# Where the expert's operands lie in on-chip memory: weights and token parts of an attention and mixture kernel moved into pools of their own

## The chip, the cores and the metric

The kernel runs on one core of a Trainium2 chip. The metric is the device time of one execution in microseconds (us), lower is better. The engines are TensorE (PE in the views; its weight loads are a row of their own, PEld), VectorE (DVE), ScalarE (ACT), GpSimd (POOL) and SyncE (SP), which only issues transfers.

## The reference: what is computed

Two stages, all in float32. The first is attention over 8 batches, 8 heads, 576 positions and 64 features: one attention over positions pooled by four, repeated back up, plus a banded attention (three neighbours to each side). The second stage takes the result as 4608 tokens of 512 features and computes a gated expert:

```python
x_prev = np.concatenate([np.zeros((B, 1, D)), x[:, :-1, :]], axis=1)
xk = mu_k * x + (1.0 - mu_k) * x_prev
xr = mu_r * x + (1.0 - mu_r) * x_prev
k = np.maximum(xk @ w_k, 0.0)          # 512 -> 1024
v = k * k @ w_v                        # 1024 -> 512
r = 1.0 / (1.0 + np.exp(-(xr @ w_r)))  # 512 -> 512
return (r * v).astype(np.float32)
```

The weights arrive as float64; the kernel reads them as pairs of 32-bit words.

## The kernel before

**Splitting into two parts.** The three products of the expert are done on PE in a 4-byte format (float32r). To keep the accuracy of float32 each operand is split into a high part and a low part (what the high part leaves over), and three products are added: high by high, high by low, low by high. A weight tile holds both parts: 2 x 512 elements of each partition, 4096 bytes, high part first. There are twenty of them: wk0 to wk7 (half c of the 1024 columns of w_k by 128-row block p, index 4c + p), wv0 to wv7, wr0 to wr3. They stay on the chip for the whole run. The token parts are made anew for each chunk: xkh and xkl, xrh and xrl (mixed tokens, 4 x 256 elements, 4096 bytes), and kh and kl (the squared activations of one 128-column block f, 256 elements, 1024 bytes).

**Chunks and units.** The 4608 tokens are taken in 18 chunks of 256 (c = 0 to 17). For a chunk PE does three kinds of units:

- a k unit (k_pe, L669, matmul at L674), one for each f = 0 to 7: 12 matmuls, p = 0 to 3 by three products. The loaded (stationary) operand is a 128x128 piece of a wk tile, the streamed (moving) operand is 256 columns of xkh or xkl. Units f = 0 to 3 use wk0 to wk3, units f = 4 to 7 use wk4 to wk7.
- an r unit (r_pe, L699, matmul at L704), two for a chunk: 12 matmuls with a 128x128 piece of xrh or xrl loaded and 512 columns of a wr tile streamed.
- a v unit (v_pe, L713, matmul at L719), one for each f: 6 matmuls with a 128x128 piece of kh or kl loaded and 512 columns of wv streamed.

So a chunk has 96 matmuls of 256 columns and 24 + 48 of 512 columns. Each matmul has a weight load of its own, which runs while the matmul before it streams; at any moment PE thus streams one tile and loads from another.

Within a steady chunk the units come in this order: k1 r0 r1 k2 k3 v0 v1 k4 v2 k5 v3 k6 v4 k7 v5 v6 v7, with k0 of the next chunk put ahead of v6 (list UNITS, L30, and L843). Behind a k unit ACT takes the relu, the square and the high part (L679, L685, L686), and DVE or POOL the low part (L693), before the v unit of the same f.

**Attention.** Between those units stand the attention's matmuls of the 32 head pairs (run_pe, L590), in float32, which end near 600 us. The first stage of the program, up to about 120 us, loads and splits the weights (weight_scale to weight_low, L281 to L323), does the first attention pairs, and fills idle PE time with dummy matmuls (keep_warm, L310 to L315, both operands from the tile nidn).

**Order.** A planner written into the kernel (class Plan, L45 to L214) orders all tasks by costs and due times, and the order on each engine is fixed by manual dependencies (in_order, L926).

**Where tiles lie.** A tile pool lays its tiles down one behind another in the order in which their tags are first used, in steps of 32 bytes, and pools stand in the order in which they are opened. There are two on-chip pools before: const (masks, the identity and the like) and work (everything else, weights and token parts among them). The small tiles between the weights (for instance mxd with 12 bytes, which takes 32) set where each one starts. Every operand piece that PE loads or streams starts a multiple of 512 bytes into its tile, so that what matters of an address below multiples of 512 is that of its tile.

Of the kernel before, what the change touches and what calls it, by code (L numbers as in the profile page):

```python
# [7 lines left out]
F32 = mybir.dt.float32  # L8
F32R = mybir.dt.float32r
# [8 lines left out]
P = 128  # L18
NP = H // 2
NF = DFF // P  # L20
CT = 256
# [195 lines left out]
@with_exitstack  # L217
def attention_moe(ctx: ExitStack, tc, q, k, v, mu_k, mu_r, w_k, w_v, w_r, band, ident, out):
    nc = tc.nc
    cp = ctx.enter_context(tc.tile_pool(name="const", bufs=1))  # L220
    wp = ctx.enter_context(tc.tile_pool(name="work", bufs=2))
    pp = ctx.enter_context(tc.tile_pool(name="psum", bufs=2, space=PSUM))
# [44 lines left out]
        return (wr if kind == "r" else wv)[i * P:(i + 1) * P, :]  # L267

    def weight_tile(key, shape, dt):
        return wp.tile([P] + shape, dt, tag="w" + key, name="w" + key, bufs=1)  # L270

    def w_k_part(p, f, h):
        c, f = divmod(f, NP)
# [2 lines left out]
    def fetch_weight(i):  # L276
        raws[i] = weight_tile(WORDER[i], [512, 2], I32)
        nc.sync.dma_start(raws[i], weight_source(WORDER[i]).rearrange("p (n w) -> p n w", w=2))
# [20 lines left out]
    def weight_high(i):  # L299
        ws[WORDER[i]] = weight_tile(WORDER[i], [2, 512], F32R)  # L300
        nc.scalar.activation(ws[WORDER[i]][:, 0, :], part32[i], AF.Copy)
# [355 lines left out]
            nc.vector.tensor_tensor(out=x[:, :, o:o + L], in0=x[:, :, o:o + L], in1=xts[b][:, :, s:s + L], op=ALU.add)  # L657

    def mix_high(c, nm):
        h = wp.tile([P, NP, CT], F32R, tag=nm + "h", name=nm + "h", bufs=2 if nm == "xk" else 1)  # L660
        nc.scalar.activation(h, mixes[c][nm], AF.Copy)
        xs[c, nm] = [h]

    def mix_low(c, nm):
        lo = wp.tile([P, NP, CT], F32R, tag=nm + "l", name=nm + "l", bufs=2 if nm == "xk" else 1)
        nc.vector.tensor_tensor(out=lo, in0=mixes[c][nm], in1=xs[c, nm][0].bitcast(F32), op=ALU.subtract)  # L666
        xs[c, nm].append(lo)

# [12 lines left out]

    def k_high(c, f):
        kk = kq[c, f]
        kh = wp.tile([P, CT], F32R, tag="kh", name="kh", bufs=4)
        nc.scalar.activation(kk, kk, AF.Square)  # L685
        nc.scalar.activation(kh, kk, AF.Copy)  # L686
        kq[c, f] = kk, kh

    def k_low(c, f):
        kk, kh = kq[c, f]  # L690
        eng = nc.gpsimd if low_on(c, f) == "POOL" else nc.vector
        kl = wp.tile([P, CT], F32R, tag="kl", name="kl", bufs=4)
        eng.tensor_tensor(out=kl, in0=kk, in1=kh.bitcast(F32), op=ALU.subtract)  # L693
        kq[c, f] = kh, kl

    def low_on(c, f):
        return "POOL" if c < KLPOOL or f in KLF else "DVE"
# [122 lines left out]
    def chunk(c):  # L820
# [5 lines left out]
        for nm, o in (("xk", 0), ("xr", 5)):  # L826
            src = f"xk32{c}" if nm == "xk" else f"dx{c}"
            for p in range(NP):

                add(*(("ACT", 0.49) if act_mix(c) else ("DVE", 0.48 * len(segs(c)))), X + o + 1 + 0.5 * p, mix_part, c, nm, (p,),  # L830
                    r=xt + [f"dx{c}", "mu"] + ([f"xkh{c}"] if nm == "xr" and c < ACTMIX else []),
                    new=[(src, "f32tmp")] if nm == "xk" and p == 0 else [], w=[src] if nm == "xr" or p else [])
            if act_mix(c):
                add("DVE", 1.22, X + o + 2.5, mix_add, c, nm, r=xt, w=[src])
            add("ACT", 1.04, X + o + 3, mix_high, c, nm, r=[src], new=[(f"{nm}h{c}", nm + "h")])
            add("DVE", 1.22, X + o + 4, mix_low, c, nm, r=[src, f"{nm}h{c}"], new=[(f"{nm}l{c}", nm + "l")])
# [7 lines left out]
        for f in range(NF):  # L844
            W = where[f"k{f}"]
            if f == NP:

                while held:
                    held.pop(0)()
            add("PE", 1.43, W, k_pe, c, f, r=[f"xkh{c}", f"xkl{c}"] + both(f"k{4 * (f // 4) + p}" for p in range(NP)),  # L850
                new=[(f"g{c}.{f}", "bank")])
            add("ACT", 0.38, W - 6, k_relu, c, f, r=[f"g{c}.{f}"], new=[(f"kk{c}.{f}", "kk")])
            add("ACT", 0.82, W - 6, k_high, c, f, w=[f"kk{c}.{f}"], new=[(f"kh{c}.{f}", "kh")])
            add(low_on(c, f), 0.42 if low_on(c, f) == "DVE" else 0.74, W - 6, k_low, c, f, r=[f"kk{c}.{f}", f"kh{c}.{f}"], new=[(f"kl{c}.{f}", "kl")])
# [126 lines left out]
```

## Time and profile before

| | us |
|---|---|
| median of three runs | 704.89 (704.68 to 708.3) |
| the profiled execution | 705.88 |
| its span, first to last instruction | 703.9 |
| PE busy within the span | 674.1 (96%) |
| PE weight loads (PEld) | 576.9 (82%) |
| DVE, ACT, POOL busy | 465.5, 439.3, 303.3 |

A matmul's record is longer than its share of PE's time, because matmuls overlap in the pipeline: one of 512 columns is recorded with 389 to 397 ns, but the next starts some 227 to 236 ns after it. What a matmul costs in a run of them is therefore read from one start to the next, not from its mean duration. In the chain of waits a piece "x12 1.43" is a run of 12 matmuls that took 1.43 us from the first start to the next piece. PEclk is the granted clock of PE in tenths of full speed; over the span it is 0.992.

### The profile page before, as it was taken

Reading aid. Unit: us, or ns where it says so; the run is one execution under the profiler, and the core shown is the slowest. Engines: PE = TensorE matmul, PEld = TensorE weight load, DVE = VectorE, ACT = ScalarE, POOL = GpSimd, SP = SyncE. Lnnn points to the kernel's source line nnn. Section 1 sums busy time; section 2 is a strip of 40 time slices with the busy share of each in tenths; the row PEclk is TensorE's granted clock in tenths of the full one; section 3 lists DMA queues with packets and bytes.
Section 4 is the critical chain, followed back from the end, with each engine's and each line's share of the span. In section 5 each row is a group of like instructions: output and inputs, shape, how many; then the busy total and the mean of one; then the engine's idle time right before and its main releaser. Section 6 shows DMA issues by size and latency. Waiting matters only on the chain.

```text
span 703.9 us, 18635 instructions
## 1 busy us (share of the span) xinstructions
PE 674.1 (96%) x7467; PEld 576.9 (82%) x7467; DVE 465.5 (66%) x855; ACT 439.3 (62%) x1095; POOL 303.3 (43%) x374
## 2 busy tenths in 40 slices
PE   7888977999999999999999999999999999999997
PEld 5565866888888888888888888888888888988986
DVE  4778987659965977498753996488748963555111
ACT  3557864777757765667665667585758575744432
POOL 5535898656453646345341555455544521000000
PEclk9999998999999999999999999999999999999999
DMA  8899997635353426242351364334351100000000
GB/s 149 181 197 273 221 148 132 124 79 116 68 114 75 107 56 128 54 93 44 87 87 52 59 115 88 88 77 104 71 101 40 53 2 31 1 30 31 1 32 31
DMA packets 221849, 62.21 MB, mean 88 GB/s; under 512 B 205122, under 2 KB 214594, under 8 KB 221762
## 3 DMA queue, kind: packets, MB, share of 16 engines
q1 hardware_dynamic: 221762, 61.01, 42.0%
q8 instruction: 59, 0.97, 0.6%
q14 instruction: 28, 0.23, 0.1%
HBM read 51.55 MB, written 9.44 MB: 87 GB/s over the span
## 4 chain that ended last, share of the span: by engine, by line
PE 69%; DVE 11%; ACT 5%; SPq 4%; POOL 4%; DMA 3%; issue 3%; DVEq 0%; POOLq 0%; ACTq 0%
PE ps_g L674 24%; PE acc L719 22%; PE ps_r L704 12%; PE ps_v L581 3%; SPq L335 3%; PE ps_a L449 2%; PE ps_v L575 2%; DMA v<-in_v_dram 1%; ACT ad L533 1%; ACT L533 1%; DVE ps_w L291 1%; PE ps_a L516 1%; DMA wv<-in_moe_w_v_dram 1%; DVE kl L693 1%; PE ps_a L509 1%
## 5 line engine op out<-in xcount | busy, mean ns | idle before, releaser
L674 PE MATMUL ps_g<-xkh,wk 128*128 128x256 f32 x1152 | 229.5, 285 | 2.9 <-ACT kk L679 2.0
L674 PEld LDWEIGHTS ps_g<-xkh,wk 128*128 128x128 f32 x1152 | 186.6, 190 | 11.4 <-ACT kk L679 4.9
L719 PE MATMUL acc<-wv,kh 128*128 128x512 f32 x576 | 181.2, 396 | 0.0
L674 PE MATMUL ps_g<-xkl,wk 128*128 128x256 f32 x576 | 162.6, 282 | 0.7 <-DVE xkl L666 0.7
L693 DVE TENSOR_TENSOR kl<-kk,kh 128x256 fp32r<-128x256 f32 x119 | 64.0, 538 | 118.0 <-ACT kh L686 110.8
L719 PEld LDWEIGHTS acc<-wv,kh 128*128 128x128 f32 x576 | 101.0, 189 | 18.9 <-issue 2.5
L674 PEld LDWEIGHTS ps_g<-xkl,wk 128*128 128x128 f32 x576 | 109.9, 191 | 3.9 <-DVE xkl L666 0.9
L719 PE MATMUL acc<-wv,kl 128*128 128x512 f32 x288 | 112.6, 391 | 0.1
L679 ACT ACTIVATE kk<-ps_g 128x256 f32<-128x256 f32 x144 | 54.5, 379 | 84.2 <-PE ps_g L674 77.9
L704 PE MATMUL ps_r<-wr,xrh 128*128 128x512 f32 x288 | 90.2, 394 | 1.7 <-POOL wr L323 1.4
L693 POOL TENSOR_TENSOR kl<-kk,kh 128x256 fp32r<-128x256 f32 x25 | 18.5, 742 | 124.2 <-PE acc L719 96.1
L719 PEld LDWEIGHTS acc<-wv,kl 128*128 128x128 f32 x288 | 54.1, 188 | 12.8 <-DVE kl L693 0.8
L686 ACT ACTIVATE kh<-kk 128x256 fp32r<-128x256 f32 x144 | 60.2, 418 | 4.6
L685 ACT ACTIVATE kk<-kk 128x256 f32<-128x256 f32 x144 | 60.1, 418 | 4.5
L704 PEld LDWEIGHTS ps_r<-wr,xrh 128*128 128x128 f32 x288 | 52.5, 188 | 12.4 <-POOL wr L323 1.8
L477 POOL TENSOR_TENSOR sm<-sm,mx 128x384 f32<-128x384 f32 x28 | 24.4, 873 | 83.1 <-DVE sd L539 60.6
L704 PE MATMUL ps_r<-wr,xrl 128*128 128x512 f32 x144 | 56.1, 390 | 0.0
L523 DVE TENSOR_REDUCE mxd<-ps_a 128x3 f32<-128x432 f32 x32 | 19.3, 604 | 48.8 <-PE ps_a L449 39.6
L422 POOL TENSOR_TENSOR v<-v 72x512 f32<-72x512 f32 x32 | 44.6, 1395 | 16.0 <-DMA v<-in_v_dram 15.8
L423 POOL TENSOR_TENSOR vd<-v 72x256 f32<-72x256 f32 x32 | 27.7, 866 | 51.0 <-PE ps_v L575 49.6
L413 POOL TENSOR_TENSOR tk<-kz 64x288 f32<-64x288 f32 (+1 forms) x56 | 41.9, 748 | 16.1 <-DVE kz L386 12.5
L533 ACT ACTIVATE ad<-ps_a,mxd 128x144 f32<-128x144 f32 x96 | 35.3, 376 | 20.3 <-DVE mxd L524 17.5
(106 smaller groups left out, 1212.5 us busy)
## 6 DMA issues: line engine op xcount, KB each, us to landing
vw<-in_v_dram SPq DMA_DIRECT2D x126, 96.0 KB
qraw<-in_q_dram SPq DMA_DIRECT2D x128, 72.0 KB
kraw<-in_k_dram SPq DMA_DIRECT2D x128, 72.0 KB
v<-in_v_dram SPq DMA_DIRECT2D x32, 288.0 KB
out_dram<-sig SPq DMA_DIRECT2D x36, 256.0 KB
wk<-in_moe_w_k_dram SPq DMA_DIRECT2D x8, 512.0 KB
wv<-in_moe_w_v_dram SPq DMA_DIRECT2D x8, 512.0 KB
wr<-in_moe_w_r_dram SPq DMA_DIRECT2D x4, 512.0 KB
```

Of the source, the lines that this page charges most:

```text
L413: nc.gpsimd.tensor_tensor(out=tk[h], in0=k4[:, :, 0:2], in1=k4[:, :, 2:4], op=ALU.add)
L422: eng.tensor_tensor(out=v4[:, :, 0:128], in0=v4[:, :, 0:128], in1=v4[:, :, 128:256], op=ALU.add)
L423: eng.tensor_tensor(out=vd, in0=v4[:, :, 0:64], in1=v4[:, :, 64:128], op=ALU.add)
L477: nc.gpsimd.tensor_tensor(out=s3, in0=s3, in1=mx[:, :, None].broadcast_to([P, 12, 32]), op=ALU.subtract)
L533: nc.scalar.activation(ad[:, t, :], ps[:, t, :], AF.Exp, scale=1.0 / 128, bias=mx[:, t:t + 1], accum_out=sd[:, t:t + 1])
L674: nc.tensor.matmul(ps, w_k_part(p, f, w), y[:, p, :], start=(m == 0), stop=(m == len(mm) - 1))
L679: nc.scalar.activation(kk, kq[c, f], AF.Relu)
L685: nc.scalar.activation(kk, kk, AF.Square)
L686: nc.scalar.activation(kh, kk, AF.Copy)
L693: eng.tensor_tensor(out=kl, in0=kk, in1=kh.bitcast(F32), op=ALU.subtract)
L704: nc.tensor.matmul(ps, y[:, p, P * t:P * t + P], ws[f"r{p}"][:, w, :], start=(m == 0), stop=(m == len(mm) - 1))
L719: nc.tensor.matmul(accs[c][t], x[:, P * t:P * t + P], ws[f"v{f}"][:, w, :], start=(f == 0 and m == 0), stop=(f == NF - 1 and m == 2))
```

## The change

Two pools are opened ahead of the others. The pool array holds the twenty weight tiles and nothing else, 20 x 4096 bytes. The pool tokens begins with an unused tile of 16 elements (64 bytes), and holds the token parts xkh, xkl, xrh, xrl, kh and kl. All other tiles stay in const and work, which now come behind. Numbers of buffers, shapes and all computation stay; on all five engines the instructions stand in the same order, with the same waits.

```diff
 def attention_moe(ctx: ExitStack, tc, q, k, v, mu_k, mu_r, w_k, w_v, w_r, band, ident, out):
     nc = tc.nc
+    ap = ctx.enter_context(tc.tile_pool(name="array", bufs=1))
+    xp = ctx.enter_context(tc.tile_pool(name="tokens", bufs=1))
+    xp.tile([P, 16], F32, name="shift")
     cp = ctx.enter_context(tc.tile_pool(name="const", bufs=1))
     wp = ctx.enter_context(tc.tile_pool(name="work", bufs=2))
...
     def weight_tile(key, shape, dt):
-        return wp.tile([P] + shape, dt, tag="w" + key, name="w" + key, bufs=1)
+        return ap.tile([P] + shape, dt, tag="w" + key, name="w" + key, bufs=1)
...
     def mix_high(c, nm):
-        h = wp.tile([P, NP, CT], F32R, tag=nm + "h", name=nm + "h", bufs=2 if nm == "xk" else 1)
+        h = xp.tile([P, NP, CT], F32R, tag=nm + "h", name=nm + "h", bufs=2 if nm == "xk" else 1)
...
     def mix_low(c, nm):
-        lo = wp.tile([P, NP, CT], F32R, tag=nm + "l", name=nm + "l", bufs=2 if nm == "xk" else 1)
+        lo = xp.tile([P, NP, CT], F32R, tag=nm + "l", name=nm + "l", bufs=2 if nm == "xk" else 1)
...
     def k_high(c, f):
-        kh = wp.tile([P, CT], F32R, tag="kh", name="kh", bufs=4)
+        kh = xp.tile([P, CT], F32R, tag="kh", name="kh", bufs=4)
...
     def k_low(c, f):
-        kl = wp.tile([P, CT], F32R, tag="kl", name="kl", bufs=4)
+        kl = xp.tile([P, CT], F32R, tag="kl", name="kl", bufs=4)
```

What this does to the addresses, in bytes past a multiple of 128 (before and after, as the two programs place their tiles):

| tiles | before | after |
|---|---|---|
| wk0, wk1, wk2 | 32 | 0 |
| wk3 to wk7, wv0 to wv7, wr0 to wr3 | 96 | 0 |
| xkh, xkl, xrh, xrl, kh, kl | 96 | 64 |
| mixed tokens before the split (dx, xk), and kk | 96 | 32 |
| idn, nidn | 0 | 64 |
| the attention's tiles | various | each moved by 64 |

The distance from a token part to the weight that it meets was 0 bytes (modulo 128) for all pairs but those with wk0, wk1 and wk2, where it was 64; it is now 64 for all. The distance between any two of the tiles that did not change pools is the same as before, modulo 128.

## The prediction

> **What bounds the kernel now.** The page first.
>
> ```profile
> span 703.9 us, 18635 instructions
> PE 674.1 (96%) x7467; PEld 576.9 (82%) x7467; DVE 465.5 (66%) x855; ACT 439.3 (62%) x1095; POOL 303.3 (43%) x374
> PE   7888977999999999999999999999999999999997
> PEclk9999998999999999999999999999999999999999
> ```
>
> PE is full in nearly every slice, at full clock. The view by stretches says from when, and the view of PE's waits what interrupts it after 120 us.
>
> ```profile
> 74.00:120.00 46.00, 36.88 (x593) 31.16 (x595) 38.06 (x57) 30.57 (x81) 41.07 (x44) 0.96 0.96 166
> 120.00:200.00 80.00, 78.65 (x981) 67.73 (x975) 61.16 (x114) 57.80 (x146) 47.58 (x59) 0.98 0.48 99
> 200.00:300.00 100.00, 98.35 (x1153) 85.01 (x1145) 69.01 (x132) 66.52 (x172) 48.81 (x60) 1.00 0.43 89
> 300.00:400.00 100.00, 100.00 (x1005) 87.82 (x1004) 70.23 (x128) 65.03 (x158) 37.09 (x46) 1.00 0.34 71
> ```
>
> ```profile
> PE ps_g L674 <- ACT kk L679: 2.0, 3, 0.8
> PE ps_t L556 <- POOL ad L544: 1.0, 2, 0.7
> ```
>
> Columns of the first are the stretch, its length, then busy time of PE, PEld, DVE, ACT and POOL. Before 120 us PE waits for loads and other engines (36.88 busy of 46). From 200 us it is busy 98 to 100 of 100, and after 120 us its longest waits sum to 2.0 and 1.0 us. So from 120 us on, a nanosecond off each matmul is a nanosecond off the end, and the question is what a matmul costs from one start to the next. The chain of waits has it for a chunk late in the program, where no attention stands between the units.
>
> ```profile
> 619.47 5.45 PE ps_r L704 x24
> 624.92 2.80 PE ps_g L674 x24
> 627.72 2.75 PE acc L719 x12
> 630.47 1.43 PE ps_g L674 x12
> 631.91 1.39 PE acc L719 x6
> ...
> 641.75 1.42 PE ps_g L674 x12
> 643.18 2.73 PE acc L719 x12
> 645.91 1.42 PE ps_g L674 x12
> 647.33 0.23 PE ps_r L704
> ```
>
> Left out are three more pairs like those at 630.47 and 631.91 (k5 to k7, v3 to v5). The chunk lasts 647.33 - 619.47 = 27.86 us: k units 2.80 + 4 x 1.43 + 2 x 1.42 = 11.36 (118.3 ns for each of 96 matmuls), r units 5.45 (227.1 ns for each of 24), v units 2.75 + 4 x 1.39 + 2.73 = 11.04 (230.0 ns for each of 48). Together 27.85.
>
> **The trial that stands in the trace already.** Units k0 to k3 load wk0, wk1 and wk2, which lie 64 bytes (modulo 128) from the streamed xkh and xkl; wk3 to wk7 lie at distance 0. So before has both layouts on the same line. The timeline of PE over k2 and k3 of the last chunk, those matmuls alone that stream xkl (one for each block p, so three matmuls from one to the next):
>
> ```profile
> 680.60 0.28 PE L674 MATMUL ps_g<-xkl,wk 128*128 128x256 f32 x1
> ...
> 681.30 0.28 PE L674 MATMUL ps_g<-xkl,wk 128*128 128x256 f32 x1
> 681.66 0.28 PE L674 MATMUL ps_g<-xkl,wk 128*128 128x256 f32 x1
> 682.02 0.28 PE L674 MATMUL ps_g<-xkl,wk 128*128 128x256 f32 x1
> ...
> 682.70 0.28 PE L674 MATMUL ps_g<-xkl,wk 128*128 128x256 f32 x1
> ```
>
> and over k4, with the first matmuls of the v unit behind it:
>
> ```profile
> 686.14 0.28 PE L674 MATMUL ps_g<-xkl,wk 128*128 128x256 f32 x1
> ...
> 687.22 0.28 PE L674 MATMUL ps_g<-xkl,wk 128*128 128x256 f32 x1
> ...
> 687.46 0.63 PE L719 MATMUL acc<-wv,kh 128*128 128x512 f32 x2
> 687.93 0.39 PE L719 MATMUL acc<-wv,kl 128*128 128x512 f32 x1
> ```
>
> In k4, at distance 0, nine matmuls take 1.08 us: 120 ns each. In k2, at distance 64, six take 0.70 us: 117 ns. Where k2 comes to wk3 (681.30 to 682.02) six take 0.72: 120 ns again. In k3, distance 64 as in k2, six take 0.68: 113.3 ns. So the distance between what is loaded and what is streamed does show, on PE, at full clock; distance 64 is never slower here than distance 0; and at distance 64 there are two rates, 117 and 113.3, of which I cannot say what selects them (k3 comes behind the disturbance by wk3, k2 comes behind r1 with none).
>
> A rule speaks against the change. The Trainium skill, page "TensorE: Matmul & The Clock Gate", section "Step-by-step: what each phase is for", says that PE reads the streamed operand and the loaded one through two independent read ports, so that loading the next weights takes nothing from the running matmul. By it both distances cost the same and the sum would be 0. The rows of k2 to k4 disagree: 113.3 to 117 against 120 ns.
>
> **The change part by part.** No instruction, byte or wait is added, taken or moved; only addresses differ.
>
> *k units.* 96 matmuls of a chunk, now 118.3 ns in the mean. After, all are at distance 64. Ends from the rows above: 113.3 (10.88 us, -0.48 for a chunk) and 117.5, the rate of k2 with its rounding (11.28, -0.08). Both rates occur, and with wk3 gone the disturbance behind which 113.3 was seen is gone too, so I take the middle, 115.4: 11.08, -0.28.
>
> *v units.* 48 matmuls. The rows give 2.73 for twelve behind k0, which loads mostly at distance 64 (227.5 ns), and 1.39 for six behind k4 to k7 (231.7). The start of a v unit pays for the state in which the k unit leaves PE: at 687.46 two matmuls take 0.47, 235 each. Ends: unchanged (0) and r's rate of 227.1 for all (10.90, -0.14). With the k units before them out of the 120 ns rate I take 227.5: 10.92, -0.12.
>
> *r units.* 24 matmuls at 227.1, with few disturbances: 0.
>
> *Which bytes.* The pieces start at 0 and 64 now, at 32 and 96 before. Alignment alone: the dummy matmuls have both operands in nidn, at 0 and at distance 0.
>
> ```profile
> 66.50:73.30 6.80, 6.80 (x32) 5.63 (x31) 1.00 1.05 131
> ```
>
> 32 of them touch 6.80 us; each is recorded with 0.39, so the spacing is about 7.19 / 32 = 225 ns (218 to 232 with one more or fewer), like r's 227.1 at 96. Aligned starts alone give nothing; I take 0.
>
> *The other engines* find their tiles moved by 64, token parts excepted. Nothing in the trace shows what this does to them, so it is bounded by their cover. Behind a k unit these follow before its v unit:
>
> ```profile
> L693 DVE TENSOR_TENSOR kl<-kk,kh 128x256 fp32r<-128x256 f32 x119 | 64.0, 538 | 118.0 <-ACT kh L686 110.8
> L679 ACT ACTIVATE kk<-ps_g 128x256 f32<-128x256 f32 x144 | 54.5, 379 | 84.2 <-PE ps_g L674 77.9
> L686 ACT ACTIVATE kh<-kk 128x256 fp32r<-128x256 f32 x144 | 60.2, 418 | 4.6
> L685 ACT ACTIVATE kk<-kk 128x256 f32<-128x256 f32 x144 | 60.1, 418 | 4.5
> ```
>
> 379 + 418 + 418 + 538 = 1.75 us, and between the end of k4 (631.91) and v4 (two v units and two k units later, 2 x 1.39 + 2 x 1.43) lie 5.64. A tenth on each of them, either way, is hidden. Without that cover, 0.17 us for each of eight units would be 1.4 us a chunk.
>
> *The sum.* -0.28 - 0.12 = -0.40 us for a chunk. Chunk 0 lies largely in the stretch up to 120 us where PE waits anyway; of the other 17 I count 16, since PE's idle 1.35 and 1.65 us between 120 and 300 show places where DVE, ACT or POOL come last and take back a part. 16 x 0.40 = 6.4 us: the span goes from 703.9 to 697.5, the profiled time from 705.88 to 699.5. That execution lies 1.0 above the median, and the same difference from the median of 704.89 gives **698.5**. Ends of the mechanism: all at the best rates, 17 x (0.48 + 0.14) = 10.5, 694.4; k2's rate and v as now, 16 x 0.08 = 1.3, 703.6.
>
> **The rivals.** *Weak form:* every k unit is entered as k2 is, at 117, and v keeps its starts: 703.6. For it: k2's rate holds over its whole undisturbed part. Against: v behind k0 is already better than behind k4. *Nothing changes,* 704.9: two independent ports, as the skill's rule has it; the difference between k2, k3 and k4 would then come from where the units stand in a chunk. Against it: within k2 the step to wk3 alone brings 120. *Slower:* the 512-column matmuls. Distance 0 is what r and v have now, and r settles at 227.1; no row shows a run of them at distance 64. If the collision that k2 shows is a matter of phase, distance 64 could hold r and v in the state that now marks only the start of a v unit, 235 ns. Then 72 x 0.235 = 16.92 against 5.45 + 11.04 = 16.49, +0.43, with k at 117.5 -0.08: +0.35 x 16 = +5.6, 710.5. It decides from 233 ns in the mean on: 229.0 now, 1.1 for k's gain, 3.0 for 3.5 us. Against: the matmuls that today load wk0 while streaming wv or wr (the last of a v or r unit ahead of k0 to k2) stand in pieces of 2.73 and 5.45 that are the shortest of their kind.
>
> **How the numbers follow.** A measurement of this kernel tells about 0.5%, 3.5 us, from no change: faster is below 701.4, slower above 708.4. The forecast, by more than that, 0.58; the weak form 0.18; nothing 0.12; the slower one 0.12, with a price between 0 and 710.5 and beyond, of which 0.02 stays within the bound. Faster 0.58, same 0.32, slower 0.10. The range of 8 in 10 reaches from 692, 2.4 below the best end since chunk 0 and rates below 113.3 may add a little, to 706, which takes in the weak form, no change and the mild part of the slower one.
>
> **What would show it.** In the profile after: twelve matmuls of a k unit in the chain at 1.36 to 1.41 instead of 1.43, the same for k0 to k3 as for k4 to k7; single v units at 1.36 to 1.37 instead of 1.39; 24 of r still 5.45; a late chunk 27.2 to 27.8 instead of 27.86; PE still 98 to 100 of 100 after 200 us. Wrong would be: k units at 1.41 and more throughout (weak form), k4 to k7 still at 1.43 (nothing), r above 5.5 (slower), or a gain in the chunks that does not reach the end because PE's waits grow.

## The result, and the profile after

The changed kernel is slower: median 709.76 us (707.25 to 712.65, 20 runs) against 705.65 for the kernel before (703.76 to 708.3, 20 runs), ratio 1.0057 (95% interval 1.0044 to 1.007). The forecast of 698.5 had the wrong sign, and the time lies above the range (692 to 706).

The page of the changed kernel first; lines of its code stand three further down than before (k units L677, r L707, v L722).

```profile
span 707.4 us, 18635 instructions
PE 680.0 (96%) x7467; PEld 577.6 (82%) x7467; DVE 465.4 (66%) x855; ACT 439.5 (62%) x1095; POOL 303.7 (43%) x374
L696 DVE TENSOR_TENSOR kl<-kk,kh 128x256 fp32r<-128x256 f32 x119 | 64.3, 540 | 119.4 <-ACT kh L689 112.1
```

DVE, ACT and POOL are as busy as before to within 0.4 us, and the last operation behind a k unit takes the same (538 ns before, 540 now). PE's busy time alone grew, by 5.9 us. The chain of waits over the late chunk, as it was shown of before:

```profile
622.16 5.60 PE ps_r L707 x24
627.76 2.82 PE ps_g L677 x24
630.58 2.80 PE acc L722 x12
633.39 1.41 PE ps_g L677 x12
634.80 1.40 PE acc L722 x6
...
646.05 2.80 PE acc L722 x12
...
650.26 0.93 PE ps_r L707 x4
```

The chunk takes 650.26 - 622.16 = 28.10 us instead of 27.86. By kind of unit:

| | before | forecast | after | a matmul after |
|---|---|---|---|---|
| k, 96 matmuls | 11.36 | 11.08 | 2.82 + 6 x 1.41 = 11.28 | 117.5 ns |
| r, 24 | 5.45 | 5.45 | 5.60 | 233.3 ns |
| v, 48 | 11.04 | 10.92 | 2.80 + 4 x 1.40 + 2.80 = 11.20 | 233.3 ns |
| chunk | 27.85 | 27.45 | 28.08 | |

The k units gained 0.08, the r units lost 0.15 and the v units 0.16. The 0.24 us of the chunk's own starts, times the 17 chunks after 120 us, are 4.1 us, as large as the difference of the medians (709.76 - 705.65 = 4.1). That they agree to the tenth is in part luck: the two profiled executions differ by 3.5 us, and the chunks with attention between their units lose less than the late one.

Summed in both traces over the starts of all matmuls from r0 of chunk 2 to r0 of chunk 17 (15 chunks), k units take 1.6 us less than before, r units 2.0 more, v units 2.4 more and the attention's matmuls the same to within 0.1: 2.9 us in all, 0.20 for a chunk. The remaining 0.5 us of the span lies ahead of and behind these chunks. PE's waits after 120 us, as the view lists them, sum to 4.3 us against 3.4 before; between r0 of chunk 2 and r0 of chunk 17 no more time goes into late starts than before.

### The profile page after: what moved, and what is told of

It is laid out like the page before. It is cut to its first block, busy times and chain, and to the rows that moved or that the text cites. A ratio compares the mean times of both kernels' runs of the same rounds, so it can differ in the third digit from the quotient of the medians.

```text
span 707.4 us, 18635 instructions
## 1 busy us (share of the span) xinstructions
PE 680.0 (96%) x7467; PEld 577.6 (82%) x7467; DVE 465.4 (66%) x855; ACT 439.5 (62%) x1095; POOL 303.7 (43%) x374
## 4 chain that ended last, share of the span: by engine, by line
PE 77%; DVE 7%; ACT 5%; POOL 4%; SPq 3%; issue 2%; DMA 1%; DVEq 0%; POOLq 0%; ACTq 0%
PE ps_g L677 25%; PE acc L722 25%; PE ps_r L707 13%; PE ps_v L584 3%; PE ps_a L452 3%; PE ps_v L578 2%; SPq L338 2%; ACT ad L536 1%; DMA v<-in_v_dram 1%; ACT L536 1%; PE ps_a L519 1%; PE ps_a L512 1%; PE ps_t L559 1%; DVE ps_w L294 1%; PE ps_t L560 1%
## 5 line engine op out<-in xcount | busy, mean ns | idle before, releaser
L677 PE MATMUL ps_g<-xkh,wk 128*128 128x256 f32 x1152 | 227.8, 284 | 3.8 <-ACT kk L682 2.2
L677 PEld LDWEIGHTS ps_g<-xkh,wk 128*128 128x128 f32 x1152 | 185.2, 189 | 12.7 <-ACT kk L682 4.9
L722 PE MATMUL acc<-wv,kh 128*128 128x512 f32 x576 | 183.6, 400 | 0.0
L677 PE MATMUL ps_g<-xkl,wk 128*128 128x256 f32 x576 | 161.2, 280 | 0.7 <-DVE xkl L669 0.7
L722 PEld LDWEIGHTS acc<-wv,kh 128*128 128x128 f32 x576 | 101.2, 189 | 20.5 <-issue 2.6
L722 PE MATMUL acc<-wv,kl 128*128 128x512 f32 x288 | 114.5, 398 | 0.0
L677 PEld LDWEIGHTS ps_g<-xkl,wk 128*128 128x128 f32 x576 | 108.7, 189 | 4.6 <-DVE xkl L669 0.9
L707 PE MATMUL ps_r<-wr,xrh 128*128 128x512 f32 x288 | 91.6, 398 | 1.8 <-POOL wr L326 1.1
L722 PEld LDWEIGHTS acc<-wv,kl 128*128 128x128 f32 x288 | 54.3, 188 | 13.6 <-DVE kl L696 0.3
L707 PEld LDWEIGHTS ps_r<-wr,xrh 128*128 128x128 f32 x288 | 52.4, 188 | 13.9 <-POOL wr L326 1.5
L707 PE MATMUL ps_r<-wr,xrl 128*128 128x512 f32 x144 | 56.9, 395 | 0.0
```

The costliest lines, as they stand in the source:

```text
L677: nc.tensor.matmul(ps, w_k_part(p, f, w), y[:, p, :], start=(m == 0), stop=(m == len(mm) - 1))
L707: nc.tensor.matmul(ps, y[:, p, P * t:P * t + P], ws[f"r{p}"][:, w, :], start=(m == 0), stop=(m == len(mm) - 1))
L722: nc.tensor.matmul(accs[c][t], x[:, P * t:P * t + P], ws[f"v{f}"][:, w, :], start=(f == 0 and m == 0), stop=(f == NF - 1 and m == 2))
```

## The experiments

Unless it says otherwise, an edit below is one to the changed kernel. One thing was overlooked and became the theory: an address modulo 128 does not tell 64 bytes ahead (at the lower address) from 64 bytes behind. From here on a distance is the start of the streamed piece minus that of the loaded piece, modulo 256. In a k unit the token part is streamed; in r and v units it is the one that is loaded. So the change puts k units at 64, but r and v units at -64, which is 192. Before, r units and all v units but v0 were at 0, k4 to k7 at 0 too, and k units with wk0, wk1 and wk2 (the trial on which the forecast rests) at 192, not at 64; wv0 and wk3 lay at 128. The theory was formed after the first four runs; their expectations still speak of distance modulo 128.

**e1, matmuls alone.** A kernel that leaves the computation out and streams and loads at 16 distances (the streamed tile starts 4096 bytes past the loaded one, so i = 0 is distance 0, and 4 * i elements are 16 * i bytes):

```python
for i in range(16):                       # widea to widep
    for m in range(24):
        a, b = 128 * (m % 8), 512 * (m % 3) + 4 * i
        nc.tensor.matmul(wide, ld[:, a:a + 128], sd[:, b:b + 512], start=True, stop=True)
# then halfa to halfp: 36 matmuls each, with sd[:, b:b + 256]
```

> A kernel with nothing but matmuls, which leaves the whole computation out: for each of 16 distances (0 to 240 bytes, steps of 16) a run of 24 matmuls of 512 streamed columns, then for the same distances runs of 36 matmuls of 256 columns; loaded pieces start at multiples of 512 bytes, streamed ones at such a multiple plus the distance. Distance theory: the spacing within a run depends on the distance modulo 128 alone; 512 columns: 227 ns at 0 and 128, 233 ns at 64 and 192; 256 columns: 120 ns at 0 and 128, 117.6 (or 113.3) at 64 and 192; between them one value or the other, perhaps a free place with 226.7 and 113.3 together. Rival (the kernel's mix of units or other engines make the difference, not the addresses): one value for all distances, near 227 and 113 to 118.

The chain of waits of this run, one piece for a distance (a is 0, e 64, h 112, i 128, m 192, n 208, p 240):

```profile
23.81 5.44 PE widea L39 x24
...
46.01 5.51 PE widee L39 x24
...
68.21 5.59 PE widei L39 x24
...
90.60 5.59 PE widem L39 x24
96.19 5.63 PE widen L39 x24
...
107.41 5.45 PE widep L39 x24
112.86 4.31 PE halfa L44 x36
...
129.90 4.24 PE halfe L44 x36
...
142.78 4.08 PE halfh L44 x36
...
163.91 4.10 PE halfm L44 x36
```

With nothing else running, 24 matmuls of 512 columns take 5.44 us at distance 0 (226.7 ns each) and 5.59 to 5.63 at most other distances (233 to 235); 240 is as good as 0 (5.45), and 64 lies between, 5.51. For 256 columns the order is another: 36 take 4.31 at 0 (119.7), 4.24 at 64 (117.8), and 4.08 and 4.10 at 112 and 192 (113.3, and 113.9 with a slower start). So the rival, one value for all, falls; and so does the distance modulo 128, since 0 and 128 differ (5.44 against 5.59), as do 64 and 192 (5.51 against 5.59; for 256 columns 4.24 against 4.10). These are the rows of the kernels: before, r at 0 with 227; after, r and v at 192 with 233.3 and k at 64 with 117.5; and the 113.3 of k3 before, at 192 (the first half of k2 before, at 192 too, ran at 117).

The Trainium skill says in the page "SBUF — State Buffer", section "Who interferes with whom", that PE and ACT never wait on anyone. The rows of e1 do not agree if that is taken to hold between PE's own two reads: nothing but PE runs there, and its matmuls go from 226.7 to 235 ns as one start is moved.

**e2, distance 0 everywhere.**

```diff
-    xp.tile([P, 16], F32, name="shift")
```

> The changed kernel without the unused tile of 64 bytes: weights and token parts all at multiples of 128, distance 0, and now aligned. Distance theory: k units at 119 to 120 ns for a matmul, r at 227, single v units at 231 to 232, a late chunk 27.9 to 28.0 us, 705 to 708 us in all, as before. Rival (starts at multiples of 64 bytes, not the distance, hold the 512-column matmuls at 233): r still 233 (5.60 for 24), a late chunk over 28.1 us, 710 us or more.

708.27 us against 705.02 beside it, ratio 1.004 (1.0026 to 1.0054), just above the 705 to 708 that were expected. Its chain:

```profile
621.91 5.47 PE ps_r L706 x24
627.38 2.87 PE ps_g L676 x24
630.25 2.75 PE acc L721 x12
```

r and v are back at the rows of before, with aligned starts, so the alignment of the start is not what slowed them. k2 and k3 lose what they had before (2.87 against 2.80): the chunk takes 27.98. Times 17 that is 2.0 us, and the medians show 3.3; the rest is open.

**e3, the same distances from other starts.** All weights 32 past a multiple of 128, all token parts 96 past:

```diff
+    ap.tile([P, 8], F32, name="start")
     xp = ctx.enter_context(tc.tile_pool(name="tokens", bufs=1))
```

> The changed kernel with all weights 32 bytes past a multiple of 128 and all token parts 96 past: distance 64 as in the change, starts off the multiples of 64 as before. Distance theory: as the changed kernel, k 117.6, r and v 233.3, a late chunk 28.1 us, 709 to 711 us. Rival (starts): r and v fall back to 227 to 231, k 113 to 118 as k0 to k3 had before, a late chunk 27.3 to 27.8, 700 to 705 us.

```profile
619.32 5.60 PE ps_r L708 x24
624.92 2.82 PE ps_g L678 x24
627.74 2.80 PE acc L723 x12
```

Row for row the changed kernel, off the multiples of 64. 707.44 us, ratio 1.0033 (1.002 to 1.0046): below the 709 to 711 that were expected of it, though the late chunk is the same 28.10. In its profiled execution it loses from r0 of chunk 2 to r0 of chunk 17 what the change loses (2.8 us against 2.9), but it comes to r0 of chunk 2 at 167.2 us, where the kernel before comes at 169.6. So the difference lies in the first stretch; why that one was shorter is not known.

**e4, the k part of the change alone.** xkh and xkl stay 64 behind, the other token parts go to the weights' offset (k at 64, r and v at 0):

```diff
+    yp = ctx.enter_context(tc.tile_pool(name="near", bufs=1))
...
+        h = (xp if nm == "xk" else yp).tile([P, NP, CT], ...)   # mix_low the same
+        kh = yp.tile([P, CT], ...)                               # kl the same
```

> The changed kernel with only xkh and xkl 64 bytes past a multiple of 128; xrh, xrl, kh and kl at multiples of 128 like the weights, so distance 64 for k units and 0 for r and v units. Distance theory: k 117.6 (11.29 us of a chunk), r 227 (5.45), v 227.5 to 230 (10.92 to 11.04), a late chunk 27.66 to 27.78, that is 702 to 704 us, faster than both kernels. Rival (the state that a unit leaves sets the next one's, whatever the distance): r and v stay at 233 behind the k units, 28.1 us and 709 to 711 us.

```profile
618.34 5.48 PE ps_r L708 x24
623.82 2.83 PE ps_g L678 x24
626.65 2.76 PE acc L723 x12
```

r and v are free again (5.48, 2.76), so the k units at 64 do not pull them to 233. But the chunk takes 27.85, as before, not 27.66 to 27.78: v still pays at its start behind k. In all 707.17 us, ratio 1.0032 (1.0015 to 1.0048). The chunks explain none of these 2 us, and the profiled execution (704.86) was the fastest of its ten, so its profile cannot show where the median's time goes. That stays open.

**e9, the other part alone** (run later): xkh and xkl at the weights' offset, the others 64 behind (k at 0, r and v at 192), by exchanging xp and yp in the diff of e4.

> The changed kernel with xkh and xkl at the weights' own offset (k units at distance 0) and xrh, xrl, kh and kl 64 bytes behind it (r and v units at distance 192): the part of the change that should cost, alone. Theory of the signed distance: k 119.4, r and v 233.3, a late chunk 11.47 + 5.60 + 11.20 = 28.27 us, 17 x 0.41 = 7 us above the kernel before, 712 to 713 us. Rival (r and v are pulled to 233 by the k units at 64): r and v back at 227 to 231, a late chunk near 28.0, 707 us.

```profile
623.56 5.60 PE ps_r L708 x24
629.16 2.86 PE ps_g L678 x24
632.02 2.80 PE acc L723 x12
```

710.96 us, ratio 1.0073 (1.0048 to 1.0099), the highest median of all, though below the 712 to 713 expected; r and v at 233 without any k unit at 64. The chunk is 651.74 - 623.56 = 28.18 by its starts. With e2 (27.98), e4 (27.85) and the change (28.10) this is a table of two by two: moving k from 0 to 64 saves 0.13 and 0.08, moving r and v from 0 to 192 costs 0.20 and 0.25. The medians, each less that of the kernel before beside it (e2 3.25, e4 2.15, the change 4.11, e9 5.11 us), have the same signs: 1.10 and 1.00 saved, 1.86 and 1.96 paid.

**e5, the period, and mixes.** Again matmuls alone: distances 256 to 496, then 12 matmuls of 256 columns and 6 of 512 by turns, at a pair of distances, four times.

> Matmuls alone, the whole computation left out: first the distances (streamed minus loaded start) 256 to 496 bytes in steps of 16, for 512 and for 256 streamed columns; then mixes of four times 12 matmuls of 256 columns at one distance and 6 of 512 columns at another, as k and v units alternate in the kernel. Theory of the signed distance modulo 256: the settled spacings of the first measurement come back (512 columns: 226.7 ns at 256 and 496, 228.9 at 320, 232.5 at 384, 233.3 at 448; 256 columns: 113.3 at 368 and 448, 117.8 at 320, 120 at 256); in the mixes twelve of 256 columns take 1.36 us at 112 and 192 and 1.41 at 64, six of 512 columns 1.36 to 1.39 at 0 and 240, 1.37 at 64 and 1.40 at 192. Rival (a longer period, or each run keeps the state that it is entered in): the values at 256 and beyond differ from those at 0 and beyond by more than 1 ns, and the mixes do not keep to the sums.

```profile
24.08 3.40 PE widea L40 x15
...
37.93 3.44 PE widee L40 x15
...
76.29 3.50 PE widep L40 x15
79.79 2.40 PE halfa L40 x20
...
108.17 2.29 PE halfm L40 x20
...
117.55 11.28 PE mixaa L40 x72
...
174.24 11.21 PE mixba L40 x72
185.45 11.11 PE mixbb L40 x72
...
207.71 11.23 PE mixbd L40 x72
...
286.21 11.07 PE mixda L40 x72
...
308.43 11.20 PE mixdc L40 x72
```

Most distances repeat after 256: 226.7 at 256 (3.40 / 15), 229 at 320, 120 at 256 and 113.3 to 115 at 448. One does not: 496 takes 3.50 (233.3) where 240 took 226.7; whether another entry or a period longer than 256 makes this is open. In the names of the mixes the first letter is the distance of the 256-column matmuls (a 0, b 64, d 192), the second that of the 512-column ones (a 0, b 16, c 64, d 192). A quarter of a row is a k unit with a v unit: 2.82 for 0 and 0, as k4 and v2 before (1.43 + 1.39); 2.81 for 64 and 192, as in the change (1.41 + 1.40); 2.80 for 64 and 0, as in e4. That one distance can hold two states shows in mixbb: by the starts of its matmuls, its four groups of twelve, all at 64, take 1.42, 1.36, 1.42 and 1.36 us, so 256-column matmuls run at 113.3 at distance 64 too. In mixdd, at 192, the first group takes 1.41 and the last 1.365. So for 256 columns 64 and 192 have the same two states, and the difference between them in e1 (4.24 and 4.10) can be one of entry. For 512 columns they stay apart in long runs, in e1 and here (229 to 230 ns at 64 and 320, 233 at 192 and 448).

**e6, the change in the mirror.** The pools are exchanged, so that token parts lie 64 ahead of the weights: k at 192, r and v at 64.

```diff
-    ap = ctx.enter_context(tc.tile_pool(name="array", bufs=1))
     xp = ctx.enter_context(tc.tile_pool(name="tokens", bufs=1))
-    xp.tile([P, 16], F32, name="shift")
+    ap = ctx.enter_context(tc.tile_pool(name="array", bufs=1))
+    ap.tile([P, 16], F32, name="shift")
```

> The changed kernel with the two pools in the other order and the unused 64 bytes ahead of the weights: token parts now lie 64 bytes ahead of the weights modulo 256, not behind. Streamed minus loaded is then 192 for k units and 64 for r and v units. Theory of the signed distance modulo 256: k 113.3 to 114 ns, r and v near 229, a late chunk 96 x 0.1138 + 72 x 0.229 = 27.4 us, 17 x 0.45 = 7.6 us below the kernel before: 697 to 698 us. Rival (distance modulo 128, where 64 ahead and 64 behind are the same): as the changed kernel, k 117.6, r and v 233.3, 28.1 us, 709 us.

```profile
617.56 5.49 PE ps_r L707 x24
623.05 2.75 PE ps_g L677 x24
...
628.54 1.39 PE ps_g L677 x12
629.93 1.37 PE acc L722 x6
...
645.11 5.49 PE ps_r L707 x24
```

702.48 us, ratio 0.9959 (0.9945 to 0.9974): faster than both kernels, though modulo 128 no distance differs from the change. r and v run at 229 (5.49 / 24), as the theory says; the chunk takes 645.11 - 617.56 = 27.55. Missed are its size (27.4) and more so the total: 17 x 0.31 would be 5.3 us, and 2.7 came. The k units start at 117 to 123 ns before they settle at 113.3. And in the chunks with attention between the units less is gained: summed over the starts of all matmuls from r0 of chunk 2 to r0 of chunk 17, k takes 4.0 us less, r 0.8 more, and v in all 0.8 more, since the v matmuls behind which the next start came late (26 against 22 of them, over 260 ns) take 1.9 more. So a part is taken back where the stream of units is interrupted; by whom was not settled.

**e7, k in the mirror, r and v at 0.**

```diff
     xp = ctx.enter_context(tc.tile_pool(name="tokens", bufs=1))
+    ap = ctx.enter_context(tc.tile_pool(name="array", bufs=1))
+    ap.tile([P, 16], F32, name="shift")
+    yp = ctx.enter_context(tc.tile_pool(name="near", bufs=1))
```

with the tiles of xp and yp as in e4.

> As the mirrored kernel for xkh and xkl alone (64 bytes ahead of the weights modulo 256, k units at 192); xrh, xrl, kh and kl at the weights' own offset, r and v units at distance 0. Theory of the signed distance: k 113.3 to 114, r 227, v 226.7 to 230 by what its start pays behind a k unit; a late chunk 10.92 + 5.45 + 10.88 to 11.04 = 27.25 to 27.4 us, 694.5 to 697.5 us. Rival (modulo 128): k 117.6 and r and v as in the kernel with the near pool at 64 behind, 27.85 us, 705 to 708 us.

```profile
615.79 5.44 PE ps_r L708 x24
621.23 2.83 PE ps_g L678 x24
...
626.77 1.41 PE ps_g L678 x12
628.19 1.36 PE acc L723 x6
```

702.14 us, ratio 0.9956 (0.994 to 0.9972), level with e6, the two fastest kernels of the study. Expected were 694.5 to 697.5 and a chunk of 27.25 to 27.4; it takes 27.62. r and v are free from their first matmul on (1.36 for six is 226.7), but the k units, at the same 192 as in e6, run at 117.5. So the state of a k unit hangs on the units around it too, in which alone e6 and e7 differ; the row mixda of e5 has the same 2.77.

**e8, the kernel before, 64 bytes further on.** An unused tile of 64 bytes ahead of everything.

> The kernel before with 64 unused bytes ahead of everything: every tile starts 64 bytes later, no distance between two tiles changes. Theory that only signed distances count: as the kernel before in every row (k4 to k7 120 ns, r 227, late chunk 27.86 us), the same time within 0.3%. Rival (where a tile starts counts by itself, which would explain the 1 to 2 us by which the aligned kernels are slower than their late chunks say): 1 us or more slower, found in the first 130 us.

705.49 us against 705.85, ratio 0.9997 (0.9983 to 1.0011); late chunk 27.86, as expected. Where tiles start does not count when all move together.

**e10 and e11, does the map predict new layouts?** e10 has xkh and xkl 64 ahead of the weights and all other token parts 64 behind (all at 192), e11 has xkh, xkl, kh and kl 64 ahead and xrh and xrl at the weights' offset, both by which pool a tile is taken from.

> xkh and xkl 64 bytes ahead of the weights, xrh, xrl, kh and kl 64 bytes behind them: every streamed start is 192 past the loaded one, modulo 256. From the mixes of bare matmuls (12 of 256 columns in 1.365 us, 6 of 512 in 1.395 when both are at 192) the theory of the signed distance gives a late chunk of 8 x 1.365 + 4 x 1.40 + 8 x 1.395 = 27.68 us: the fastest k units of all and r as slow as in the change; 17 x 0.18 = 3 us below the kernel before, 702 to 703. Rival (the state in the full kernel does not follow the mixes): k at 117.6 and r, v at 233.3, 28.1 us and 709 us.

> xkh, xkl, kh and kl 64 bytes ahead of the weights, xrh and xrl at the weights' own offset: k units at 192, r at 0, v at 64. Theory of the signed distance, with the rows of the two mirrored kernels: k 1.39, r 5.45, v 1.37 for six, a late chunk of 8 x 1.39 + 5.45 + 8 x 1.375 = 27.5 us, 701 to 702.5 us, about as the mirrored kernels. Rival (a new phase at the entry from r): k2 and k3 as slow as 1.41 each, 27.6 us, no better than either.

e10, then e11, from their chains:

```profile
619.19 5.60 PE ps_r L709 x24
...
630.32 1.42 PE ps_g L679 x12
631.74 1.40 PE acc L724 x6
633.14 1.38 PE ps_g L679 x12
```

```profile
617.74 5.46 PE ps_r L708 x24
...
628.79 1.41 PE ps_g L678 x12
630.20 1.39 PE acc L723 x6
```

Both miss. e10: 708.12 us, ratio 1.0038 (1.0023 to 1.0052); r is at 233 as said, but k units go 1.42 and 1.38 by turns instead of 1.365, and the chunk takes 27.90. e11: 704.09 us, ratio 0.9986 (0.9971 to 1.0), hardly to be told from the kernel before, chunk 27.87; r is at 227 as said, but v, at 64 as in e6, takes 1.39 instead of 1.37, and k 1.41 instead of 1.39. For e11 the better row was at hand: mixdc of e5, with k at 192 and v at 64, has 2.80 for a pair, as e11 has, where the rows of e6 that the expectation took give 2.76. So the same distances gave two states in e6 and e11. The signed distance sets where runs of 512 columns settle; it does not say in which state a short unit starts, and sums of single rows do not carry that.

## Why the prediction was wrong

*What bounds the kernel* held: a change in the spacing of matmuls reached the end, 2.9 of the 3.5 us between the profiled executions in 15 of the chunks, with the other engines as busy as before.

*The step that failed* is "The trial that stands in the trace already", where it took the distance modulo 128 and let the pair in k0 to k3 stand for all pairs of the change. Modulo 256 that pair was at 192; the change put k units at 64 and r and v units at 192. e1 shows that the two differ with nothing else running (5.51 against 5.59 us for 24 matmuls of 512 columns), and e6 decides: the mirror image, the same modulo 128, is 0.4% faster than before where the change is 0.57% slower. The sentence "distance 64 is never slower here than distance 0" was true of the rows quoted, all of 256 columns; for 512 columns 0 is the best place of all (e1: 5.44).

*k units.* Forecast 115.4, measured 117.5, the weak end, -0.08. The middle between 117 and 113.3 was taken without a row at the new distance and without knowing what selects the rate. At 64 the late k units of the change, of e3 and of e4 all take 1.41 to 1.42 us; that 64 can hold 113.3 shows only in e5 (mixbb), among units that the kernel does not have.

*v units.* Forecast -0.12, measured +0.16. That v would follow k out of its slow start was argued from v behind k0; in the change v is at 192, where single units (1.40) and pairs (2.80) both run at 233.3, so there is no slow start to leave behind.

*r units.* Forecast 0, measured +0.15. This was costed at nothing for having few disturbances now, without a row at the new distance.

*The slower rival* named the place (the 512-column matmuls), the direction and the point from which it decides (233 ns in the mean); 233.3 came where it had put 235, and its 710.5 was near the 709.76 measured. It had 0.12, since "no row shows a run of them at distance 64" was read as if nothing spoke for it. What spoke against it were single matmuls at the end of a unit, and one matmul does not show what a run settles at. But r and v units are 16.49 of a chunk's 27.86 us: what most of the chunk would do had no row at all, and that should have held far more of the chance than a rule inferred from k units.

*The rule of two independent ports*, as a forecast of no change, would have given 704.9; between the change and e6, and within e1, nothing but addresses differs, and the times do, so it does not hold here in that form. *Alignment alone* and *the other engines* were rightly costed at nothing (e2 and e3 for r and v; e8).

What stays open: by which mechanism the distance acts (only the addresses and the spacings were seen; that PE's two reads disturb each other is inferred, since no run streams without loading), what selects the state in which a k unit starts, and the 1 to 3 us by which e2, e4, e6, e7 and e10 are slower, and e3 and e11 faster, than 17 late chunks would make them.

## What to carry to other kernels

A natural trial inside a trace holds for the shapes and the exact values that it has: before it is carried over, ask what it cannot tell apart (here a sign, a longer period, and a second shape that does three fifths of the work). Where an address effect is suspected, a kernel of bare matmuls that steps one start through 256 bytes gives a first map in one run; it should be made for every width that the kernel streams, and in more than one order, since a distance can hold more than one state. Then measure the layout in the kernel itself, since short units need not reach the settled rates of long runs (e10 and e11).

## What the runs showed of the hardware that was not expected

- With float32r operands the spacing of back-to-back matmuls changes with the distance between streamed and loaded piece: 226.7 to 235 ns for 512 columns, 113.3 to 120 ns for 256, in steps as small as 16 bytes, with different best places for the two widths (0 against 112 and 192).
- The same distance can hold two states: 256-column matmuls at 64 took 1.42 and 1.36 us for twelve by turns (e5, mixbb), and k units at 192 settled at 113.3 ns (e6) and at 117.5 (e7). At 240 512 columns took 226.7 ns in e1, and at 496, which is 240 modulo 256, 233.3 in e5.
- No run settled below 226.7 and 113.3 ns, and moving everything by 64 bytes changed nothing (ratio 0.9997).
